# Wider score tiles, a split value product and one load moved up in a fused attention and SwiGLU kernel

## The chip, the cores and the metric

The kernel runs on one core of one Trainium2 chip. Its metric is the device time of one execution in microseconds, from the median of several runs. Five engines work side by side: PE (TensorE: matmuls, and their weight loads, which the profile lists apart as PEld), DVE (VectorE), ACT (ScalarE), POOL (GpSimd) and SP (SyncE). POOL also issues the loads, and SP the transposing copies and the stores.

## The reference

Softmax attention over 8 batches, 12 heads, 448 positions and head size 64, and then a gated feed-forward block over the 3584 resulting rows of 768 channels. Inputs and output are float32; the kernel computes with float16 operands and float32 accumulation.

```python
def _attn_ref(q, k, v):                      # (8, 12, 448, 64) each
    scores = np.matmul(q, k.transpose(0, 1, 3, 2)) / np.sqrt(q.shape[-1])
    scores = scores - np.max(scores, axis=-1, keepdims=True)
    attn = np.exp(scores)
    attn = attn / (np.sum(attn, axis=-1, keepdims=True) + 1e-09)
    return np.matmul(attn, v)

def _moe_ref(x, w_gate, w_val, w_out):       # x (3584, 768); 768 -> 1536 -> 768
    g = x @ w_gate
    silu = g * (1.0 / (1.0 + np.exp(-g)))
    return silu * (x @ w_val) @ w_out
```

## The kernel before

**Pairs, chunks and visits.** Heads are taken in 48 pairs, six pairs to a batch. A pair's scores are built transposed, keys on the partitions. For the pairs 0 to 11 the 448 keys are four chunks of 112 (`qk`, L234: two matmuls per chunk, one per head, 64 rows by 128 columns of weights). From pair 12 (`SPLIT`) on they are three chunks of 128 keys (`qk_split`, L249), and a remaining 64 keys. The remainders of two neighbouring pairs share one tile, called the rest (`qk_rest`, L265): the first 64 of its partitions hold the first half of the queries, the other 64 the second half. Each score tile is turned into `E` by one exponential on ACT.

After six pairs in an opening loop, the program runs through 54 *visits* that a list `plan` fixes. A visit issues up to three chunks, then what is due of an older couple of pairs (`todo`), and then feed-forward steps of an earlier batch. From pair 12 on, two kinds are due for each couple: "sums" (softmax sums, then reciprocals on DVE) and "both" (the value products of both pairs). For "both", `pv_rest` (L281) starts the two accumulators `acc[0]` and `acc[1]`, one for each half of the queries, and `pv_split` (L297) adds the three chunks to the first half and then to the second, each followed by a scaling on DVE into `X` (`scaled_half`, L312).

**Column tiles.** `qk_split` writes its 128 output partitions in four column tiles of 32: eight matmuls of 64 rows by 32 columns for a chunk, with a weight load for each; `qk_rest` has sixteen. In a visit with something due, the feed-forward matmuls are split by four in the same manner (`mm`, L396, under `tiled[0]`), and show as 128\*32 on line L401. In the other visits they are whole (128\*128, L398). The sums and value products are 128\*32 always.

**Feed-forward.** One step of `ffn1_steps` is a gate group `gp` in a buffer of the pool `ps_s` (3 buffers, shared with the score tiles), a tanh on ACT, a value group `vp` in a buffer of `ps_f` (2 buffers, shared with `acc` and `op`), and two products on DVE. `run_fv` runs such a step in its two halves. `ffn2_steps` gives the projection groups `op`: in the first block all three groups with the first half of the output weights (`wo[0]`), and then three with the second (`wo[1]`). A new block's steps are added by `add_block` in the visits in which its batch's last value product is made.

**Loads.** POOL issues them in program order. `wq` tells at which pair's visit the early ones are issued: the third group of values and `wo[0]` at pair 6, `wo[1]` at pair 7. From pair 8 on, each even pair loads q and k of the two pairs that are six further (`load_qk16`, `LA = 6`), so pair 8 loads 14 and 15, in four DMAs on line L136. `prep(pr + 3)` arranges a pair's q and k on POOL (L196 for pair 11, four copies on L182 from pair 12 on) and has SP transpose them into `qkT` (L199, L186). `double_rest` (L157) copies a part of the values on POOL. Each load on POOL's queue waits for the landing of the one eight before it.

```python
        wq = {
            0: [("qk", 6), ("g", 0), ("v", 0)],
            1: [("qk", 8), ("g", 1), ("v", 1)],
            3: [("qk", 10), ("V", 2), ("g", 2), ("v", 2)],
            4: [("g", 3), ("v", 3), ("qk", 12)],
            6: [("V", 3), ("o", 0)],
            7: [("o", 1)],
        }
```

The visits that matter most below, by the time of their first score matmul in the profiled execution: visit 8 at 63.07 us (chunks of pair 11), visit 9 at 69.17 (the last chunk of pair 11, two of pair 12), visit 10 at 72.89 (one of pair 12, two of 13), visit 11 at 79.36 (the last of 13, the rest, the first of 14), visit 12 at 84.51 (two of 14, the first of 15), visit 14 at 100.38.

Of the kernel before, what the change touches and what calls it, by code (L numbers as in the profile page):

```python
# [20 lines left out]
LA = 6  # L21
# [8 lines left out]
def kernel(  # L30
# [11 lines left out]
    B, H, S, D = q.shape  # L42
# [7 lines left out]
    NPAIR = B * NHP  # L50
# [4 lines left out]
    H2 = S // 2  # L55
    RS = 64
# [189 lines left out]
            )  # L246
        nc.scalar.activation(E[pr][:, c], s[0:P, :, 0:S], AF.Exp, scale=sm_scale)  # L247

    def qk_split(pr, c):  # L249
        if c == 0:  # L250
            E[pr] = ep.tile([128, NC, 2, S], FP16, tag="E", name="E")
        t = qkT[pr]
        s = ps_s.tile([128, 2, 512], FP32, tag="s")
        for j in range(4):
            for hx in range(2):
                nc.tensor.matmul(  # L256
                    s[ts(j, 32), hx, 0:S],
                    lhsT=t[ts(hx, 64), c, ts(j, 32)],
                    rhs=t[ts(hx, 64)].rearrange("p c q -> p (c q)")[:, S : 2 * S],
                    start=True,  # L260
                    stop=True,
                )
        nc.scalar.activation(E[pr][:, c], s[:, :, 0:S], AF.Exp, scale=sm_scale)  # L263

    def qk_rest(p0):  # L265
        s = ps_s.tile([128, 2, 512], FP32, tag="s")
        for i in range(2):
            t = qkT[p0 + i]
            for j in range(4):
                half = j // 2  # L270
                for hx in range(2):
                    nc.tensor.matmul(
                        s[ts(j, 32), hx, ds(i * H2, H2)],
                        lhsT=t[ts(hx, 64), 3, ds(j % 2 * 32, 32)],
                        rhs=t[ts(hx, 64)].rearrange("p c q -> p (c q)")[:, ds(S + half * H2, H2)],
                        start=True,
                        stop=True,
                    )
        nc.scalar.activation(E[p0 + 1][:, 3], s[:, :, 0:S], AF.Exp, scale=sm_scale)  # L279
# [14 lines left out]
                    )  # L294
        return acc

    def pv_split(p0, acc):  # L297
        for half in range(2):
            for c in range(3):
                for t in range(2):  # L300
                    for j in range(4):
                        g, r = divmod(p0 + j // 2, GP)
                        nc.tensor.matmul(  # L303
                            acc[half][ts(j, 32), ds(t * H2, H2)],
                            lhsT=v16[g][:, 2 * r + j % 2, c + 1, :].rearrange("p (d t) -> p t d", t=2)[:, t],
                            rhs=E[p0 + j // 2][:, c, j % 2, ds(half * H2, H2)],
                            start=False,
                            stop=(c == 2 and t == 1),
                        )
            scaled_half(p0, half, acc[half])  # L310

    def scaled_half(p0, half, acc):  # L312
        b, hp = divmod(p0, NHP)
        kk, bb = divmod(b, NB)
        if kk not in X:
            X[kk] = xp.tile([128, NCB, NB * S], FP16, tag="X", name="X")
        nc.vector.tensor_tensor(  # L317
            X[kk][:, hp : hp + 2, ds(bb * S + half * H2, H2)],
            acc[:, 0:S].rearrange("p (t q) -> p t q", t=2),
            R[p0][:, ds(half * H2, H2)].unsqueeze(1).to_broadcast([128, 2, H2]),  # L320
            ALU.mult,
        )
# [170 lines left out]
    def block(i):  # L493
        kk, odd = divmod(i, 2)
        c0, n = (384, 512) if odd else (0, 384)
        hts = hp_.tile([128, NFB, 512], FP16, tag="h")
        return ffn1_steps(kk, c0, n, hts), ffn2_steps(kk, c0, n, hts, i == 0, i == B - 1), n

    with tc.manual_schedule():
# [21 lines left out]
            3: [("qk", 10), ("V", 2), ("g", 2), ("v", 2)],  # L521
            4: [("g", 3), ("v", 3), ("qk", 12)],
            6: [("V", 3), ("o", 0)],
            7: [("o", 1)],
        }

        def emit(item):
# [10 lines left out]
        def pop_deferred(n=1):  # L538
            for _ in range(n):
                if deferred:  # L540
                    deferred.pop(0)()

        fvq = []
        oq = []
        count = {}

        def add_block(i, visits):
            f1, f2, n = block(i)
            oq.extend(ffn2_wait)
            ffn2_wait.clear()  # L550
            fvq.extend([(f1, NCB * n / 2400.0)] * NFB)
            own = [(f2, NFB * OH / 2400.0)] * (2 * (n // 128))
            (oq if i == 0 else ffn2_wait).extend(own)
            count.update(visits=visits, fv=NFB, o=len(oq), at=0, more=NFB - visits)

        def run_fv():
            gen, t = fvq.pop(0)
            for _ in range(2):
                next(gen)
                pop_deferred()  # L560
            return 2 * t

        def run_o():
            gen, t = oq.pop(0)
            next(gen)
            pop_deferred(2)
            return t

        def run_budget(budget):
            while (fvq or oq) and budget > 0:  # L570
                budget -= run_fv() if fvq else run_o()
            return budget
# [7 lines left out]
        for pr in range(FIRST):  # L580
# [24 lines left out]
            if pr in (2, 4):  # L605
                pop_deferred(1)
                halves = [pv(pr - 2, 0)]
# [4 lines left out]
        halves = [pv(p4, t) for t in range(2)]  # L612
# [3 lines left out]
        for p0 in range(FIRST, NPAIR, 2):  # L616
            at = len(units)
# [9 lines left out]
        while g < len(units) or queue:  # L627
            n = 2 if g < (WIDE - FIRST) * NC else 3
            todo = []
# [11 lines left out]
        def product(kind, p0):  # L641
            if kind == "sums":
                pop_deferred(99)
                deferred.extend(recips(p0, sums(p0)))
            elif kind == "both":
                pop_deferred(99)
                pv_split(p0, rests.pop(p0))
            else:
                if kind == 0:
                    pop_deferred(99)  # L650
                scaled(p0, kind, pv(p0, kind))

        def score(pr, c):
            if c == "rest":
                qk_rest(pr)
            elif pr >= SPLIT:
                qk_split(pr, c)
            else:
                qk(pr, c)

        rests = {}

        carry = 0.0
        for x, (chunks, todo) in enumerate(plan):
            for pr, c in chunks:
                score(pr, c)
            for _, kind, p0 in todo:
                if kind == "both":
                    rests[p0] = pv_rest(p0)
            end = min([y for y in adds if y > x] + [len(plan) + 1])  # L670
            if x == 0:
                for t in range(2):
                    scaled(p4, t, halves[t])
                add_block(0, end)
            turn2 = None
            entered = [pr for pr, c in chunks if c == 0]
            for pr in entered:
                if pr >= SPLIT:
                    double_rest(pr)
                if NPE <= pr + 3 < NPAIR:  # L680
                    prep(pr + 3)
                if pr % 2 == 0 and 14 <= pr + LA < NPAIR:
                    load_qk16(pr + LA)
                if pr % GP == 0 and 4 <= pr // GP + 1 < NGRP:
                    load_v(pr // GP + 1)
            for pr, c in chunks:
                if c == 2 and pr < NPE - 2:
                    prep(pr + 2)()
            any_p = len(todo)
            if x in adds and x > 0:  # L690
                while todo:
                    product(*todo.pop(0)[1:])
                add_block(adds[x], end - x)
            while todo:
                product(*todo.pop(0)[1:])
            for pr in entered:
                for w in wq.pop(pr, []):
                    emit(w)
            tiled[0] = bool(any_p) and (not chunks or chunks[0][0] >= TILED)
            if adds[max(y for y in adds if y <= x)] < 2:  # L700
                carry = run_budget(left() / (end - x) + carry)
            else:
                at, n = count["at"], count["visits"]
                no = share(count["o"], at, n)
                nf = 1
                if no and count["more"] > 0:
                    o_left = sum(1 for y in range(at, n) if share(count["o"], y, n))
                    extra = -(-count["more"] // o_left)
                    nf += extra
                    count["more"] -= extra  # L710
                count["at"] += 1
                for step in range(no if not any_p else 0):
                    run_o()
                for y in range(nf):
                    if fvq:
                        run_fv()
                for _ in range(no if any_p else 0):
                    run_o()
            tiled[0] = False
        run_budget(1e9)  # L720
        pop_deferred(99)
        add_block(B - 1, 1)
# [33 lines left out]
```

The softmax here doesn't subtract the row's maximum and nothing guards it: scores larger than these inputs give would overflow.

## Time and profile before

| what | value |
|---|---|
| time, median of 6 runs (lowest to highest) | 463.03 us (461.44 to 466.65) |
| profiled execution, its own time | 463.45 us |
| its span, first to last instruction | 461.6 us |
| instructions in the span | 19197 |
| PE busy | 445.1 us (96%) |
| DVE, ACT, POOL busy | 238.4, 227.1, 152.3 us |
| granted TensorE clock, mean | 0.998 |

The span is 1.85 us shorter than the time of that execution. PE is busy nearly all the time, so what counts is where it isn't, and the steps between its groups of matmuls. A line of the profile names the engine and the source line, what is written and read, and the shape: "64\*32 64x448" is a matmul with 64 rows and 32 columns of weights and 448 columns streamed. "Idle before, releaser" tells what ended the engine's wait; "issue" means that nothing that the profile shows was waited for.

### The profile page before, as it was taken

What the parts mean: (1) busy time and instruction counts of PE and PEld (TensorE: products, weight loads), DVE (VectorE), ACT (ScalarE), POOL (GpSimd) and SP (SyncE); (2) the same over time, 40 slices, a digit from 0 to 9 for tenths busy, and PEclk for the clock granted to TensorE, in tenths of its full rate; (3) what the DMA queues carried; (4) which work ended last, traced back from release to release, by engine and by line L of the source; (5) the groups of instructions that cost most, each with busy time, mean ns of one, the idle gap of its engine ahead of it and who ended that gap; (6) DMA issues with size and microseconds to landing.
All of it is one profiled execution on the core that took longest, in us unless ns stands there. A gap on an engine that the chain in (4) does not pass through costs nothing.

```text
span 461.6 us, 19197 instructions
## 1 busy us (share of the span) xinstructions
PE 445.1 (96%) x8816; PEld 259.8 (56%) x8816; DVE 238.4 (52%) x374; ACT 227.1 (49%) x335; POOL 152.3 (33%) x320
## 2 busy tenths in 40 slices
PE   8899998979999999999999999999999999999996
PEld 3355555455456676565557665555546666544564
DVE  2765763547476545746366374566357455354200
ACT  6986656535545445545353455633545542222222
POOL 8554806945536061811527125520400000000000
PEclk9999999999999999999999999999999999999999
DMA  9999999997847166933919639743322102100133
GB/s 131 195 200 201 188 178 148 214 147 88 103 70 99 46 94 110 145 45 77 141 35 119 98 59 136 111 49 77 44 64 58 27 14 70 36 1 0 36 103 104
DMA packets 86289, 44.57 MB, mean 97 GB/s; under 512 B 51264, under 2 KB 82752, under 8 KB 86208
## 3 DMA queue, kind: packets, MB, share of 16 engines
q0 software_dynamic: 46592, 23.37, 41.9%
q1 hardware_dynamic: 39376, 19.77, 23.9%
q8 instruction: 69, 1.13, 1.0%
q10 hardware_dynamic: 240, 0.20, 0.1%
q14 instruction: 12, 0.10, 0.1%
HBM read 47.19 MB, written 11.01 MB: 126 GB/s over the span
## 4 chain that ended last, share of the span: by engine, by line
PE 80%; DMA 13%; POOL 2%; issue 1%; DVE 1%; ACT 1%; ACTq 0%; POOLq 0%
PE vp L401 15%; PE gp L401 15%; PE op L401 13%; PE op L398 8%; PE gp L398 6%; PE vp L398 6%; PE acc L303 5%; PE s L256 5%; DMA wg<-in_moe_w_gate_dram 5%; DMA k<-in_k_dram 5%; PE acc L362 3%; DMA wv<-in_moe_w_val_dram 3%; PE acc L288 1%; DMA qkT<-qk 1%; PE wp L107 1%
## 5 line engine op out<-in xcount | busy, mean ns | idle before, releaser
L429 DVE SCALAR_TENSOR_TENSOR t<-sg,gp 128x384 f32<-128x384 f32 (+1 forms) x96 | 58.7, 612 | 98.6 <-ACT sg L417 98.6
L417 ACT ACTIVATE sg<-gp 128x384 f32<-128x384 f32 (+1 forms) x96 | 52.5, 547 | 97.6 <-PE gp L401 63.9
L263 ACT ACTIVATE E<-s 128x896 f16<-128x896 f32 x108 | 92.7, 921 | 15.1 <-PE s L256 14.8
L401 PE MATMUL gp<-X,wg 128*32 128x384 f16 (+1 forms) x1632 | 89.4, 350 | 0.7 <-issue 0.4
L401 PE MATMUL vp<-X,wv 128*32 128x384 f16 (+1 forms) x1632 | 88.8, 349 | 0.0
L462 ACT ACTIVATE osb<-op 128x384 f32<-128x384 f32 (+1 forms) x57 | 27.8, 488 | 106.8 <-PE op L401 81.8
L401 PE MATMUL op<-wo,hts 128*32 128x384 f16 x1728 | 77.2, 326 | 1.3 <-issue 0.9
L386 DVE RECIPROCAL R<-ssb 128x112 f32<-128x112 f32 x92 | 73.5, 829 | 0.8
L432 DVE SCALAR_TENSOR_TENSOR hts<-t,vp 128x384 f16<-128x384 f32 (+1 forms) x96 | 59.6, 621 | 11.2 <-DVE t L429 1.4
L401 PEld LDWEIGHTS <-wv 128*32 128x32 f16 x1632 | 47.3, 97 | 29.0 <-issue 0.3
L401 PEld LDWEIGHTS <-hts 128*32 128x32 f16 x1728 | 49.7, 97 | 24.0 <-issue 2.3
L401 PEld LDWEIGHTS <-wg 128*32 128x32 f16 x1632 | 46.0, 97 | 26.2 <-issue 2.1
L136 POOL DMA_DIRECT2D vt<-in_v_dram x24 | 16.0, 675 | 117.9 <-PE acc L303 117.9
L247 ACT ACTIVATE E<-s 112x896 f16<-112x896 f32 x48 | 40.4, 924 | 6.7 <-PE s L240 6.3
L398 PE MATMUL op<-wo,hts 128*128 128x384 f16 (+1 forms) x252 | 40.2, 319 | 0.0
L398 PE MATMUL gp<-X,wg 128*128 128x512 f16 (+1 forms) x168 | 37.7, 360 | 0.7 <-ACT E L279 0.7
L398 PE MATMUL vp<-X,wv 128*128 128x512 f16 (+1 forms) x168 | 37.6, 360 | 0.0
L182 POOL COPY qk<-k 128x384 f16<-128x384 f16 x72 | 28.7, 398 | 24.4 <-DMA qkT<-qk 22.5
L383 DVE COPY ssb<-acc 128x448 f32<-128x448 f32 x23 | 14.4, 624 | 38.7 <-PE acc L371 31.9
L317 DVE TENSOR_TENSOR X<-acc,R 128x448 f16<-128x448 f32 x36 | 21.7, 625 | 23.2 <-PE acc L303 23.2
L256 PE MATMUL s<-qkT 64*32 64x448 f16 x864 | 30.0, 353 | 3.8 <-issue 2.3
L398 PEld LDWEIGHTS <-hts 128*128 128x128 f16 x252 | 23.9, 98 | 16.0 <-issue 1.7
(60 smaller groups left out, 352.7 us busy)
## 6 DMA issues: line engine op xcount, KB each, us to landing
out_dram<-osb SPq DMA_DIRECT2D x42, 192.0 KB, 2.7
wg<-in_moe_w_gate_dram POOLq DMA_DIRECT2D x8, 288.0 KB, 11.1
wv<-in_moe_w_val_dram POOLq DMA_DIRECT2D x8, 288.0 KB, 11.4
q<-in_q_dram POOLq DMA_DIRECT2D x18, 128.0 KB, 4.4
k<-in_k_dram POOLq DMA_DIRECT2D x18, 128.0 KB, 5.7
wo<-in_moe_w_out_dram POOLq DMA_DIRECT2D x2, 1152.0 KB, 18.6
vt<-in_v_dram POOLq DMA_DIRECT2D x12, 192.0 KB, 5.2
q<-in_q_dram POOLq DMA_DIRECT2D x18, 96.0 KB, 4.0
```

What stands on the lines that cost most here:

```text
L182: nc.gpsimd.tensor_copy(qk7[rows, c0 : c0 + n].rearrange("p c h d -> p h c d"), src[rows, :, x0 : x0 + n])
L247: nc.scalar.activation(E[pr][:, c], s[0:P, :, 0:S], AF.Exp, scale=sm_scale)
L256: nc.tensor.matmul(s[ts(j, 32), hx, 0:S], lhsT=t[ts(hx, 64), c, ts(j, 32)], rhs=t[ts(hx, 64)].rearrange("p c q -> p (c q)")[:, S : 2 * S], ...
L263: nc.scalar.activation(E[pr][:, c], s[:, :, 0:S], AF.Exp, scale=sm_scale)
L303: nc.tensor.matmul(acc[half][ts(j, 32), ds(t * H2, H2)], lhsT=v16[g][:, 2 * r + j % 2, c + 1, :].rearrange("p (d t) -> p t d", t=2)[:, t], ...
L386: lambda i=i: nc.vector.reciprocal(rt[:, ts(i, P)], ssb[:, ts(i, P)]) for i in range(4)
L398: nc.tensor.matmul(dst, lhsT=lhsT, rhs=rhs, start=start, stop=stop)
L401: nc.tensor.matmul(dst[ts(j, 32), :], lhsT=lhsT[:, ts(j, 32)], rhs=rhs, start=start, stop=stop)
L417: nc.scalar.activation(sg[:, 0:n], gp[:, 0:n], AF.Tanh, scale=0.5)
L429: nc.vector.scalar_tensor_tensor(t1[:, 0:n], sg[:, 0:n], 1.0, gp[:, 0:n], ALU.add, ALU.mult)
L432: nc.vector.scalar_tensor_tensor(hts[:, fb, 0:n], t1[:, 0:n], 0.5 * HS, vp[:, 0:n], ALU.mult, ALU.mult)
L462: nc.scalar.activation(osb[:, ds(m0, w)], op[:, 0:w], AF.Copy, scale=1.0 / HS)
```

## The change

It has three parts. The column tiles of `qk_split` and `qk_rest` get a width per visit: 32 where a "both" is due, else 64 where the visit has a rest, else 128. The second half of `pv_split` is no longer issued right after the first: it is put in a list `second` and issued behind the next gate group (or by `finish()`, where a block is added, where no feed-forward step follows, and at the end of a visit). And q and k of the pairs 14 and 15 are loaded at pair 7, with `wo[1]` moved to pair 8.

```diff
-    def qk_split(pr, c):
+    def qk_split(pr, c, cols):
...
-        for j in range(4):
+        for j in range(128 // cols):
             for hx in range(2):
                 nc.tensor.matmul(
-                    s[ts(j, 32), hx, 0:S],
-                    lhsT=t[ts(hx, 64), c, ts(j, 32)],
+                    s[ts(j, cols), hx, 0:S],
+                    lhsT=t[ts(hx, 64), c, ts(j, cols)],
...
-    def qk_rest(p0):
+    def qk_rest(p0, cols):
...
-            for j in range(4):
-                half = j // 2
+            for j in range(128 // cols):
+                half, at = divmod(j * cols, RS)
                 for hx in range(2):
                     nc.tensor.matmul(
-                        s[ts(j, 32), hx, ds(i * H2, H2)],
-                        lhsT=t[ts(hx, 64), 3, ds(j % 2 * 32, 32)],
+                        s[ts(j, cols), hx, ds(i * H2, H2)],
+                        lhsT=t[ts(hx, 64), 3, ds(at, cols)],
...
-    def pv_split(p0, acc):
-        for half in range(2):
+    def pv_split(p0, acc, halves):
+        for half in halves:
...
-            7: [("o", 1)],
+            7: [("qk", 14)],
+            8: [("o", 1)],
...
             for _ in range(2):
                 next(gen)
+                while second:
+                    second.pop()()
                 pop_deferred()
...
-                pv_split(p0, rests.pop(p0))
+                acc = rests.pop(p0)
+                pv_split(p0, acc, (0,))
+                second.append(lambda: pv_split(p0, acc, (1,)))
...
+        def finish():
+            while second:
+                second.pop()()
...
+            cols = 64 if any(c == "rest" for _, c in chunks) else 128
+            if any(kind == "both" for _, kind, _ in todo):
+                cols = 32
             for pr, c in chunks:
-                score(pr, c)
+                score(pr, c, cols)
...
-                if pr % 2 == 0 and 14 <= pr + LA < NPAIR:
+                if pr % 2 == 0 and 16 <= pr + LA < NPAIR:
                     load_qk16(pr + LA)
...
+                finish()
                 add_block(adds[x], end - x)
...
+                if not fvq or not nf:
+                    finish()
...
             tiled[0] = False
+            finish()
```

More of the change, by code (lines that the diff above doesn't have):

```diff
@@ L541, in pop_deferred @@
                     deferred.pop(0)()
+        second = []
         fvq = []
@@ L651, in product, with score @@
                 scaled(p0, kind, pv(p0, kind))
-        def score(pr, c):
+        def finish():
+            while second:
+                second.pop()()
+        def score(pr, c, cols):
             if c == "rest":
-                qk_rest(pr)
+                qk_rest(pr, cols)
             elif pr >= SPLIT:
-                qk_split(pr, c)
+                qk_split(pr, c, cols)
             else:
```

## The prediction

> **What bounds the kernel now.** First the page's busy row: PE fills 96% of the span, no other engine more than 52%. So time is gained or lost only where PE stands still, or between its groups. The DMA row shows the engines nearly full for nine slices (some 104 us), then not.
>
> ```profile
> PE 445.1 (96%) x8816; PEld 259.8 (56%) x8816; DVE 238.4 (52%) x374; ACT 227.1 (49%) x335; POOL 152.3 (33%) x320
> ...
> DMA  9999999997847166933919639743322102100133
> ```
>
> Next, PE's waits from 60 to 112 us, where the moved load acts. Three carry the case: one for pair 14's `qkT`, two for "issue".
>
> ```profile
> PE s L256 <- issue: 2.3, 1, 2.3
> PE s L256 <- DMA qkT<-qk: 1.4, 1, 1.4
> PE acc L288 <- DVE hts L432: 0.7, 2, 0.4
> PE op L401 <- issue: 0.7, 1, 0.7
> ```
>
> The chain of waits shows where pair 14 was held up: its last k load is issued at 52.66, behind both output-weight loads, and lands at 74.38; the copies follow, the transpose lands at 81.33, and PE starts at once.
>
> ```profile
> 47.68 2.05 POOL wo L170 x2
> ...
> 52.66 21.72 DMA k<-in_k_dram
> 74.59 1.20 POOL qk L182 x3
> 76.16 5.17 DMA qkT<-qk
> ```
>
> Last, PE's timeline at the 2.3 us "issue" wait: it stops after 7 of a chunk's 8 matmuls, with every operand there.
>
> ```profile
> 100.38 0.38 PE L256 MATMUL s<-qkT 64*32 64x448 f16 x7
> 103.10 0.72 PE L256 MATMUL s<-qkT 64*32 64x448 f16 x17 [2.34 <-issue]
> ```
>
> Counting PE's and PEld's records, this stop is before number 3263. Four more such stops end at 76.67, 94.44, 254.00 and 258.27, at numbers 2239, 3007, 10175 and 10431: all leave 191 when divided by 256. The trace also has instruction packets of 16384 bytes on queue 8 (at 74.32, 92.05, 99.92, 251.52, 255.94), and each stop ends 1.3 to 1.7 us after one has finished. So PE runs out of instructions at a 256-instruction boundary when that packet comes late. Against undisturbed spacing the five cost 0.85 + 0.31 + 2.53 + 0.43 + 0.60 = 4.7 us.
>
> **The change, part by part.** *Wider tiles.* By the visit list, 56 chunks in 19 visits go from 8 matmuls to 2; in 7 visits 12 chunks go to 4, and 7 rests from 16 to 8. With their weight loads that is 672 + 96 + 112 = 880 fewer of 17638 PE instructions. Does the array gain? The trace has both widths beside 32-column work:
>
> ```profile
> 54.12 0.74 PE L240 MATMUL s<-qkT 64*128 64x448 f16 x6
> 54.80 0.94 PE L335 MATMUL acc<-E,vt 112*32 112x448 f16 x16
> ...
> 314.29 0.76 PE L256 MATMUL s<-qkT 64*32 64x448 f16 x24
> 314.98 0.75 PE L362 MATMUL acc<-E,ones 128*32 128x448 f16 x12
> ```
>
> Three chunks take 0.68 us wide and 0.69 narrow: the eight narrow matmuls already run at once. A change of shape costs 0.10 to 0.12 us beyond the last group's streaming (into 64\*128: 0.11, into 64\*32: 0.11, out: 0.105 and 0.115). Worth 0.01 us in each of 26 visits, plus one change of shape (0.107) that goes in visit 9, where pairs 11 and 12 now have one width: -0.35 us. No trace row has 64\*64 in this use; between its two neighbours it lies at nothing, and I bound it at +-0.05 us in 7 visits, +-0.35. A rule speaks against wide tiles: the Trainium skill, "TensorE: Matmul & The Clock Gate", section "LDWEIGHTS (loading the stationary operand)", gives columns/1.2 ns, so 107 ns for 128 columns against 27 for 32. With no matmul in flight to hide it after a change of shape, 19 x 80 + 7 x 27 ns = +1.7 us (an estimate from that page). The rows say 93 ns for a 64x128 load and 90 for a 64x32, and the first matmul starts 5 ns after the first load in both. I take the rows: nothing.
>
> *Instructions.* This is where the width can pay. "Runtime: NRT & Kernel Launch", section "Instruction fetch mechanics", calls a 16 KiB boundary mostly hidden; by that, 880 instructions are worth nothing. The trace puts 4.7 us on five boundaries. Fewer instructions mean 3.4 of 69 boundaries less, which alone is 0.2 us; but they also move the boundaries and spread them over more time. At the 100 us stop, 164 instructions are saved by then, so the boundary falls into visit 14's feed-forward, some 3.7 us of work later, while the packet is asked for (when the previous boundary is passed) only 2.9 us later. At 76 us, 60 saved put it 1.2 us later. Deferring half of a value product helps the same way: 48 instructions in 0.58 us move behind a gate group that uses 48 in 0.97 to 1.29. Bounds: -4.7 (all gone) and +2 (as many stops as before, and one of the longest size nearly added). I take -2.6: most of the three stops before 104 us (-3.0), half of the two at 254 and 258 (-0.5), and +0.9 for new ones.
>
> *Second half behind a gate group.* No matmul is added, and no shape changes, since a "both" visit's feed-forward is 128\*32 too. The 0.58 us of the second half gave cover: the gate group takes the buffer of the visit's first score tile, whose exponential ends 0.14 us before the second half starts (in 14 of 17 visits; more in the others). A release takes 0.05 us, so the gate group, 0.58 us earlier, still has 0.09 to spare. `acc[1]` is freed some 1 to 1.3 us later; the next user of its buffer is the second value group, which starts 1.9 us or more after that half. Only where one step is followed by `op` (visits 50 and 53) it is nearly even: 0.05 each. DVE's scaling of the second half is ahead of the step's two products, as before. POOL's value loads wait for these products (117.9 us in all, 9 times), with transposes behind them in POOL's queue; but from pair 16 on a transpose lands 11 us or more before its use, so 1.3 us hurts nobody. In the five visits that add a block nothing is deferred. Sum: 0.
>
> *Pair 14's loads.* Four DMAs (two q, two k) go ahead of `wo[1]`, and with it ahead of pair 11's two POOL copies. What becomes early: after `wo[0]` (62.0, from 47.68 + 14.3 us to landing) the four take 74.38 - 71.7 = 2.7 us, so pair 14 lands at 64.7 instead of 74.4, and its 1.62 us stall (1.44 in the wait list, with the step into the group) can go. What becomes late:
> - Pair 11's copies. The four issues cannot start before 48.7, and the second must wait for the load eight before it (landed at 49.7). They end at 51.7, the copies at 52.9: the transpose is issued 2.0 us later than 50.93. It landed 1.88 us ahead of its use: a stall of about 0.2.
> - The transposes of 12 and 13 come 0.8 us later from POOL and follow in SP's queue, where they landed 5.5 us apart while `wo` was moving. Pair 13 had 0.83 us to spare: 0 to 1.3, I take 0.6.
> - `wo[1]` lands 2.7 us later, at 74.4, and pair 14's transpose now shares its transfer (a transpose alone takes 2.9 us): 74.4 to 77.3. The fourth projection, its first user, started at 74.35, and at 75.0 with the two stalls above: 0 to 2.3, I take 0.2.
> - Pair 14 itself, behind 13 in SP's queue, lands near 79.4, when PE comes for it. Pair 15 waits, in POOL's order, for a `double_rest` that needs values loaded behind `wo[1]`; its transpose landed at 84.31 with 0.59 to spare, and PE would come 0.5 to 1.5 us sooner: +0.3.
> Sum: -1.62 + 0.2 + 0.6 + 0.2 + 0.3 = -0.3, with ends at -1.6 and +3.
>
> Total: -0.35 - 2.6 + 0 - 0.3 = -3.25 us. The profiled execution took 463.45 us (span 461.6), 0.42 over the median of 463.03; the stalls are counted in that execution, so I subtract from it: 460.2 us.
>
> **The rivals.** *B: the stops only move.* Boundaries come as often within 5%, and DMA stays full until 104 us, so other groups are hit for the same 4.7 us. For it: the stops at 254 and 258 lie where DMA is not full. Against: the long one depends on one packet in one jam. 463.45 - 0.65 = 462.8.
>
> *C, slower: the transposes and `wo[1]` come late.* Place: PE at the fourth projection. `wo[1]` was 23.0 us on its way; issued at 52.9 it would land at 75.9, and with pair 14's transpose inside at 78.8. For it: transposes issued during `wo` took 10.3, 12.0 and 14.5 us, against a median of 5.2. Against: the bytes ahead of it grow by 2.7 us only. With the stalls of 11 and 13 grown to 1.4 together, PE would come at 75.6 and wait 3.2: 1.4 + 3.2 - 1.62 - 0.35 = +2.6, and with the instruction stops merely moved 466.1. It decides once `wo[1]` lands about 1.2 us after PE has come for it, stops unchanged.
>
> *D: gate groups wait for the score buffer.* If exponentials end over 0.09 us later than now in the 13 deferred visits, each waits; 0.3 each is +3.9: 464.1. Against: chunks, shapes and ACT's order in those visits are unchanged.
>
> *E: all goes well.* Pair 14's stall goes without a new one, the stops nearly vanish: 463.45 - 0.35 - 1.6 - 4.0 = 457.5.
>
> **How the numbers follow.** The forecast 0.47, B 0.22, C 0.12, D 0.07, E 0.12. Faster by over 0.5% means under 460.7, slower over 465.3 (half a percent is about what a measurement of this kernel can tell from no change). The forecast lies just under that bound: 0.39 of it faster, 0.08 same. E is faster; B and D are same, with 0.02 of them slower; C is 0.11 slower and 0.01 same. Faster 0.51, same 0.36, slower 0.13. The range from 457.4 to 465.0 leaves out most of C and the outer half of E.
>
> **What would show it.** Right: 480 matmuls on L256 (now 864) and 232 on L272 (now 288), 16758 PE instructions; pair 14's score chunk without a DMA wait near 79 us; "issue" waits of PE under 2.5 us in sum; the PE groups of sums visits with unchanged spacing; no PE wait of `gp` for `E`. Wrong: an "issue" wait of over 2 us anywhere before 110; `op` L401 waiting for `wo`, or `s` for `qkT`, by over 1.5 us in sum between 60 and 90 us; shape changes into or out of 64\*128 or 64\*64 of over 0.15 us.

## The result: 0.23% faster, where 0.6% was forecast as likeliest

The changed kernel takes 460.7 us (median of 35 runs) beside 461.82 for the kernel before (72 runs, which hold the six shown at first): a ratio of 0.9977, 95% interval 0.9964 to 0.9990. That is faster by more than its own noise, 1.1 us, and less than the 2.8 us that the forecast put between its 460.2 and the first median. The two first profiled executions lie further apart, 463.45 and 460.47 us (spans 461.6 and 458.7), and that difference is a part of the answer. All ratios, intervals and counts of clocks leave out the few slow runs, over 1.5% above the fastest of their kernel. A ratio is not the quotient of the medians shown.

The page's busy and DMA rows after the change: 440 matmuls and as many weight loads fewer, the same work on the other engines, and DMA engines full for about as long.

```profile
PE 444.3 (97%) x8376; PEld 257.1 (56%) x8376; DVE 237.6 (52%) x374; ACT 226.5 (49%) x335; POOL 152.3 (33%) x320
...
DMA  9999999998678086934839558823323102100143
```

PE's waits from 60 to 112 us after the change. PE still waits for `qkT`, now twice, and the two "issue" waits have become one of 0.3.

```profile
PE s L256 <- DMA qkT<-qk: 1.3, 2, 0.7
PE acc L288 <- DVE hts L432: 0.7, 2, 0.4
PE vp L401 <- issue: 0.3, 1, 0.3
PE op L401 <- DVE X L349: 0.3, 1, 0.3
```

PE's timeline says whose transposes these are. At 74.03 it is pair 13, at 84.36 pair 15; pair 14's first chunk at 80.15 runs without a wait.

```profile
72.92 0.36 PE L256 MATMUL s<-qkT 64*128 64x448 f16 x2
74.03 0.55 PE L256 MATMUL s<-qkT 64*128 64x448 f16 x4 [0.74 <-DMA qkT<-qk]
...
80.15 0.36 PE L256 MATMUL s<-qkT 64*64 64x448 f16 x4
...
84.36 0.36 PE L256 MATMUL s<-qkT 64*128 64x448 f16 x2 [0.54 <-DMA qkT<-qk]
```

The chain shows why 15 is late. Pair 14's last k load lands at 66.07, 8.3 us earlier than before, and its copies follow at once. Then POOL stands for 8.44 us, until the values behind the second output weights land and the copy on L157 can run; pair 15's copies are behind it.

```profile
51.46 14.61 DMA k<-in_k_dram
...
66.28 1.20 POOL qk L182 x3
...
67.82 8.44 issue
...
76.28 0.30 POOL vt L157
76.63 1.20 POOL qk L182 x3
...
78.20 6.11 DMA qkT<-qk
```

POOL's timeline names the landing that the chain shows as "issue":

```profile
76.28 0.29 POOL L157 COPY vt<-vt 64x128 f16<-64x128 f16 x1 [8.46 <-DMA vt<-in_v_dram]
```

A sums visit with wide tiles, to be held against the two timelines of before: three chunks and the change of shape take 0.67 us.

```profile
311.38 0.74 PE L256 MATMUL s<-qkT 64*128 64x448 f16 x6
312.05 0.75 PE L362 MATMUL acc<-E,ones 128*32 128x448 f16 x12
```

And the longest stop of PE in this execution, now at 197 us, inside a gate group that the second half of a value product follows at 198.13:

```profile
195.41 0.39 PE L401 MATMUL gp<-X,wg 128*32 128x512 f16 x3
197.04 1.46 PE L401 MATMUL gp<-X,wg 128*32 128x512 f16 x21 [1.24 <-issue]
198.13 0.75 PE L303 MATMUL acc<-E,vt 128*32 128x224 f16 x22
```

Counted as in the prediction (records of PE and PEld in order, the excess over undisturbed spacing wherever the number leaves 191 when divided by 256), the stops of this execution are 0.29, 0.51 and 1.41 us, 2.2 in sum, where the first profile of before had 4.7.

That these stops are late instructions can be tested on all 14 profiles listed below. The packets of 16384 bytes on queue 8 are counted in order, and each is set beside its own boundary: packet 1 beside number 447, packet 2 beside 703, and so on by 256. PE passes 917 such boundaries, and never sooner than 1.22 us after the end of the boundary's own packet. Each of the 56 stops there that cost over 0.15 us ends 1.2 to 1.9 us after that packet.

### The profile page after: what moved, and what is told of

It reads as the page before. It is cut to its first block, busy times and chain, and to the rows that moved or that the text cites. A ratio compares the mean times of both kernels' runs of the same rounds, so it can differ in the third digit from the quotient of the medians.

```text
span 458.7 us, 18316 instructions
## 1 busy us (share of the span) xinstructions
PE 444.3 (97%) x8376; PEld 257.1 (56%) x8376; DVE 237.6 (52%) x374; ACT 226.5 (49%) x335; POOL 152.3 (33%) x320
## 4 chain that ended last, share of the span: by engine, by line
PE 80%; DMA 12%; issue 3%; ACT 2%; DVE 1%; POOL 1%; ACTq 0%; POOLq 0%
PE vp L401 15%; PE gp L401 15%; PE op L401 13%; PE op L398 8%; PE gp L398 6%; PE vp L398 6%; PE acc L303 5%; PE s L256 5%; DMA k<-in_k_dram 3%; PE acc L362 3%; DMA wv<-in_moe_w_val_dram 3%; DMA q<-in_q_dram 3%; DMA vt<-in_v_dram 2%; ACT E L247 1%; DMA qkT<-qk 1%
## 5 line engine op out<-in xcount | busy, mean ns | idle before, releaser
L401 PE MATMUL gp<-X,wg 128*32 128x384 f16 (+1 forms) x1632 | 89.3, 350 | 1.5 <-issue 1.2
L401 PE MATMUL vp<-X,wv 128*32 128x384 f16 (+1 forms) x1632 | 89.0, 349 | 0.3 <-issue 0.3
L401 PE MATMUL op<-wo,hts 128*32 128x384 f16 x1728 | 76.9, 326 | 0.4 <-DVE X L349 0.3
L401 PEld LDWEIGHTS <-hts 128*32 128x32 f16 x1728 | 49.7, 97 | 22.9 <-issue 1.4
L401 PEld LDWEIGHTS <-wv 128*32 128x32 f16 x1632 | 46.1, 97 | 28.7 <-issue 0.8
L401 PEld LDWEIGHTS <-wg 128*32 128x32 f16 x1632 | 45.2, 97 | 27.9 <-issue 2.9
L256 PE MATMUL s<-qkT 64*32 64x448 f16 (+2 forms) x480 | 29.5, 353 | 1.3 <-DMA qkT<-qk 1.3
```

The costliest lines, as they stand in the source:

```text
L256: nc.tensor.matmul(s[ts(j, cols), hx, 0:S], lhsT=t[ts(hx, 64), c, ts(j, cols)], rhs=t[ts(hx, 64)].rearrange("p c q -> p (c q)")[:, S : 2 * S],
L401: nc.tensor.matmul(dst[ts(j, 32), :], lhsT=lhsT[:, ts(j, 32)], rhs=rhs, start=start, stop=stop)
```

## The experiments

Ratios are against the kernel before, run beside each: its median was 462.28 us beside before2, after2, width_only and load_only, 462.31 beside width_defer, defer_only, copies_first and width_defer_shift, and 462.52 beside before_shift, after_shift, width_defer_shift_again and width_defer_shift2. So medians of different rows are not to be compared. The shifted versions with wide tiles have 7 to 9 runs each, the others 14 to 35. Columns on the right come from one profiled execution each: the stops at instruction boundaries, and the waits between 60 and 90 us for a transpose or for the second output weights (both as excess over undisturbed spacing, which is up to 0.3 us more than the wait that a view shows).

| kernel | median us | ratio, 95% interval | stops, us | data waits, us |
|---|---|---|---|---|
| before, first profile | 461.82 | 1 | 4.7 | 1.6 |
| before2 | 462.84 | 1.0006 (0.9984 to 1.0027) | 3.8 | 1.1 |
| defer_only | 462.18 | 1.0000 (0.9985 to 1.0014) | 3.3 | 1.3 |
| load_only | 464.29 | 1.0046 (1.0027 to 1.0066) | 5.1 | 3.8 |
| before_shift | 463.49 | 1.0017 (0.9997 to 1.0036) | 8.7 | 0.2 |
| after, first profile | 460.70 | 0.9977 (0.9964 to 0.9990) | 2.2 | 1.6 |
| after2 | 460.95 | 0.9975 (0.9954 to 0.9997) | 7.6 | 0.6 |
| width_only | 462.20 | 0.9988 (0.9963 to 1.0013) | 2.4 | 2.5 |
| width_defer | 461.46 | 0.9969 (0.9948 to 0.9991) | 3.9 | 2.5 |
| copies_first | 462.15 | 0.9992 (0.9969 to 1.0015) | 1.1 | 4.2 |
| after_shift | 459.79 | 0.9955 (0.9932 to 0.9978) | 1.3 | 0.8 |
| width_defer_shift | 458.26 | 0.9937 (0.9913 to 0.9961) | 1.4 | 1.5 |
| width_defer_shift_again | 459.56 | 0.9931 (0.9905 to 0.9956) | 0.6 | 1.6 |
| width_defer_shift2 | 460.30 | 0.9946 (0.9914 to 0.9978) | 1.8 | 2.0 |

**before2 and after2: the same two kernels, profiled again.** No edit.

> The kernel before, unchanged, for a second profile. Theory (the record's sum is right in kind, but the profiled execution before was an unlucky one): PE's instruction stops, 4.7 us in the first profile, come out nearer to 3 us here, still at numbers that leave 191 when divided by 256; pair 14 again waits about 1.5 us for its transpose. Rival (the stops are a fixed cost of this program): again five stops at the same five numbers, 4.7 us within 0.3.

> The changed kernel, unchanged, for a second profile. Theory: stalls for the transposes of pairs 13 and 15 again, 1.6 us in sum, and instruction stops of 1 to 3 us at other places than in its first profile; time 0.1 to 0.4% under the kernel before. Rival (stops fixed): again 0.29, 0.51 and 1.41 us near 78, 97 and 197 us.

The stops came at the same five numbers in before2, but with other sizes: the one at number 3263 was 0.89 us instead of 2.53, the one at 2239 was 1.39 instead of 0.85. So the rival, a fixed cost of the program, is out. In after2 they are 7.6 us in sum, from 2.2; the profiled execution was 465.22 us, among the slowest of its 22. PE's waits from 60 to 300 us in after2:

```profile
PE vp L401 <- issue: 2.8, 2, 1.9
PE gp L401 <- issue: 1.7, 1, 1.7
PE op L401 <- issue: 1.3, 1, 1.3
```

So the numbers at which a stop can fall are the same in every profile; how long it is differs from one execution to the next by as much as 1.6 us (at 3263 before, at 3007 after). One profile is one draw. The theory's 1 to 3 us for after2 was too narrow, and pair 13's stall didn't come back (its transpose landed 0.48 us ahead of its use).

**width_only.** The load order and the value products are put back:

```diff
-            7: [("qk", 14)],
-            8: [("o", 1)],
+            7: [("o", 1)],
...
-                pv_split(p0, acc, (0,))
-                second.append(lambda: pv_split(p0, acc, (1,)))
+                pv_split(p0, acc, (0, 1))
```

(with `14 <= pr + LA` as in the kernel before.)

> Only the column tiles get their width by the visit; value products whole, loads in the old order. Theory (width is what pays, by shape changes and fewer instructions): -0.35 us from shape changes and 0.5 to 1.5 us from stops, so 0.2 to 0.4% faster; the stall of pair 14 (1.5 us) stays. Rival (the gain is the load's): no difference, within 0.1%.

Inconclusive: 0.12% faster, with an interval that holds no gain as well as 0.37%. The wait for pair 14 was 2.4 us here, and in 8 of its 14 runs the mean granted clock was 0.997 or less (the last section shows where that is lost), in the kernel before in 25 of 152.

**load_only.** Of the change only the load order is kept; `cols = 32` in all visits, value products whole.

> Only pair 14's loads go ahead of the second output weights; score tiles all 32 wide, value products whole. Theory: pair 14's stall of 1.6 us is replaced by stalls for 13 (0.9) and 15 (0.7) and perhaps 0.2 for 11: time the same within 0.15%. Rival (the gain is the load's): 0.2 to 0.4% faster.

Slower by 0.46%, so neither the theory nor its rival. POOL's timeline shows what the four issues of pair 14 do to pair 11's copies (L196): the second q load waits 1.41 us for the load eight before it, and the copies start at 53.07, where they started at 49.72 in the kernel before.

```profile
48.18 1.03 POOL L170 DMA_DIRECT2D wo<-in_moe_w_out_dram  x1 [1.30 <-issue]
49.21 0.63 POOL L136 DMA_DIRECT2D q<-in_q_dram  x1
51.26 0.61 POOL L136 DMA_DIRECT2D q<-in_q_dram  x1 [1.41 <-DMA wv<-in_moe_w_val_dram]
51.86 1.23 POOL L136 DMA_DIRECT2D k<-in_k_dram  x2
53.07 0.64 POOL L196 COPY qk<-q 112x512 f16<-112x512 f16 x1
```

PE's waits from 60 to 112 us show what it cost: 1.9 for pair 11, and 1.4 for the pairs 13 and 15.

```profile
PE s L256 <- issue: 2.6, 1, 2.6
PE s L240 <- DMA qkT<-qk: 1.9, 1, 1.9
PE s L256 <- DMA qkT<-qk: 1.4, 2, 0.8
```

Pair 14 no longer waits. In the changed kernel's own two profiles pair 11 came through with 0.66 and 1.32 us to spare. Here it did not: the transpose was issued 1.0 to 1.3 us later still, at 54.28, and took 10.7 us to land where it had taken 9.2 in both.

**width_defer.** The change without the load's part.

> Widths by visit and the split value product, loads in the old order. Theory: 0.2 to 0.4% faster than the kernel before, so as good as the whole change or better, with pair 14's stall of 1.1 to 1.6 us still there. Rival (the load carries the gain): no faster than the kernel before.

0.31% faster, as good as the whole change. The load adds nothing to the time that could be measured, though pair 14 waits 2.2 us in this profile. It may show in the clock: 8 of 20 runs here had a mean granted clock of 0.997 or less, of the changed kernel's 56 only 2.

**defer_only.** Of the change only the second half is moved.

> Only the second half of the value products goes behind the first gate group; tiles 32 wide, loads in the old order. Theory: no wait of a gate group for E, none of a projection for acc, shape changes and instruction count as before, stops at the same numbers and of 3.8 to 4.7 us: time the same within 0.15%. Rival (spreading the instructions thins the stops): 0.2% or more faster, with the stops at 254 and 258 us gone.

No difference, to within 0.15%, and no new wait. Between 60 and 300 us the list of PE's waits has none of a gate group of the tiled visits (L401) for `E`, and none of a projection for the split product's `acc`. The one wait of a gate group for `E` is that of a whole group, which the kernel before has too:

```profile
PE gp L398 <- ACT E L279: 0.7, 1, 0.7
```

The stops, 3.3 us, came out under the 3.8 to 4.7 expected. Of the two late ones one was absent (254 us), the other 0.61 us.

**copies_first.** Pair 14's loads back at pair 8, behind pair 11's copies, with the second output weights still behind them:

```diff
-            7: [("qk", 14)],
             8: [("o", 1)],
...
-                if pr % 2 == 0 and 16 <= pr + LA < NPAIR:
+                if pr % 2 == 0 and 14 <= pr + LA < NPAIR:
```

> The changed kernel with one order mended: pair 14's loads stay at pair 8, where pair 11's copies go ahead of them, and the second output weights follow at pair 8. Theory (the moved load was paid for by pair 11's copies standing behind its four issues): pair 11's transpose is issued near 51 us again instead of 53.3, lands before its use with over 1 us to spare, pair 13's stall (0.9) goes, pair 14's stays away, and 0.5 us or so is left at pair 15: 1 us faster than the changed kernel, 0.4 to 0.5% faster than the kernel before. Rival (the transposes are held up by the weights' traffic alone, whatever POOL's order): pair 13 waits as in the changed kernel, time equal to it.

The theory's first steps hold: pair 11's transpose is issued at 50.87, the pairs 11, 13 and 14 do not wait. But the time is that of the kernel before, not 0.4 to 0.5% under it. The second output weights were issued at 53.77 and landed at 77.78, and the fourth projection waited for them; then pair 15 was 2.0 us late. PE's waits from 60 to 112 us:

```profile
PE op L401 <- DMA wo<-in_moe_w_out_dram: 2.1, 1, 2.1
PE s L256 <- DMA qkT<-qk: 1.8, 1, 1.8
```

This is the place of the prediction's rival C, in another kernel. With its 1.1 us of stops, the fewest but one, it still gained nothing. Its matmuls stand in the same order as those of the changed kernel and of width_defer. Yet the boundary at which three profiles of those two stopped for 1.4 to 1.9 us, inside the gate group at 197 to 200 us (number 7359), was passed without a stop in this execution:

```profile
198.38 1.61 PE L401 MATMUL gp<-X,wg 128*32 128x512 f16 x24
```

**width_defer_shift, and the same again.** The start's dummy matmuls are cut in four. The columns streamed stay the same, and 72 instructions more stand ahead of all else:

```diff
-        for _ in range(n):
-            nc.tensor.matmul(wp[:], lhsT=warm[:, 0:128], rhs=warm[:], start=True, stop=True)
+        for _ in range(4 * n):
+            nc.tensor.matmul(wp[:, 0:128], lhsT=warm[:, 0:128], rhs=warm[:, 0:128], start=True, stop=True)
```

> As width_defer, with the twelve dummy matmuls of the start cut in four each (128 columns instead of 512), which adds 72 PE instructions ahead of everything else: every instruction boundary moves 72 instructions earlier in the work. Theory (the stops are a lottery of boundary against traffic): the stops come at other places of the work, their sum changes by 1 to 2 us either way against width_defer, and the time with it, while waits for data stay. Rival (stops sit where DMA is jammed, wherever the boundary falls): the sum stays within 0.5 us.

> The fastest version once more, for more runs and a second profile. Theory: 0.4 to 0.7% faster than the kernel before, stops of under 2 us in sum, none near 199 us. Rival (its few runs were lucky): 0.3%, as width_defer.

0.63% and 0.69% faster than the kernel before: the best version here, and better than the changed kernel, whose interval ends at 0.36%. Laid beside each other matmul by matmul, the profile of width_defer_shift ends 3.4 us ahead of that of width_defer: it gains 1.9 at 199 us, 1.75 between 92 and 98 and about 1 around 80 and 84, loses 0.9 at 102 and 0.7 at 303 to its own stops, and keeps step elsewhere to 0.4 us. So nearly all of the difference is stops and data waits. The stop that cost width_defer 1.8 us at 199 us is absent. PE's timeline there, of width_defer:

```profile
197.23 0.39 PE L401 MATMUL gp<-X,wg 128*32 128x512 f16 x3
199.28 1.05 PE L401 MATMUL gp<-X,wg 128*32 128x512 f16 x16 [1.66 <-issue]
```

and of width_defer_shift, at the same group, whole:

```profile
194.79 0.65 PE L303 MATMUL acc<-E,vt 128*32 128x224 f16 x20
195.27 1.47 PE L401 MATMUL gp<-X,wg 128*32 128x512 f16 x24
```

In the second profile of it the longest wait from 60 to 300 us is that for pair 14 (1.3 us); the one "issue" wait in that list is 0.4.

**width_defer_shift2.** `8 * n` dummies of 64 columns: 168 instructions more.

> As width_defer, with each dummy cut in eight (64 columns): +168 instructions. Theory (lottery): a third set of stops, at places of the work that neither width_defer nor width_defer_shift has; their sum anywhere from 1 to 5 us, and a time from 0.1 to 0.6% under the kernel before. Rival (cutting the dummies helps by itself): as fast as width_defer_shift or faster, with the start ending earlier.

0.54% faster. One stop of 1.8 us at 100.7 us, none near 199; pair 15 waited 1.9. The start ends no earlier.

**before_shift.** The same cut into four in the kernel before.

> The kernel before with the start's twelve dummy matmuls cut in four each (+72 PE instructions ahead of all else, the array's time the same). Theory (a lottery of boundary against traffic): the boundary that stopped PE at 101 to 103 us falls 72 instructions earlier in the work, into the last value group before it, with the same traffic: a stop there of 1 us or more again; time the same within 0.2%. Rival (cutting the dummies helps by itself): 0.3% faster or more.

No gain; if anything slower. So the cut dummies do not help by themselves. The stop near 102 us was 3.5 us long (2.53 and 0.89 in the two profiles without the cut), and others came at 76, 198, 202 and 296 us. Its waits from 60 to 300 us:

```profile
PE gp L401 <- issue: 3.6, 2, 3.4
PE acc L303 <- issue: 1.4, 2, 0.8
PE acc L362 <- issue: 1.0, 1, 1.0
```

**after_shift.** The cut into four in the changed kernel.

> The changed kernel with the same 72 instructions more. Theory: the stop near 197 to 200 us (1.4 and 1.9 us in the two profiles of the changed kernel) is gone, as in width_defer_shift; the stalls of pairs 13 and 15 stay; 0.2 to 0.4% under the changed kernel, 0.4 to 0.6% under the kernel before. Rival (the width and the deferral carry it, not the boundaries): time equal to the changed kernel, 0.2% under the kernel before.

0.45% faster than before, as the theory had it, and the stop near 197 us is absent. The interval holds the changed kernel's own ratio (0.9977), so the rival, that it is no faster than that kernel, is not excluded. Pair 13's stall was absent in this execution, pair 15's was 0.8 us.

## Why the prediction was right, and where its sum was not

The range and the direction held, and the likeliest time of 460.2 us was 0.5 off. That closeness is luck: the sum started 1.6 us too high, at the time of one execution, and took 2.1 us too much off, 3.25 where the change took 1.1. Point by point:

*Wider tiles on the array: -0.35.* Right in kind. Into 64\*128 costs 0.11 us as before; out of it into 128\*32 costs 0.095 where 64\*32 cost 0.115; 64\*64 into 128\*128 costs 0.105, so the unseen shape lies between its neighbours. The change of shape in visit 9 is gone. That sums to -0.5 us. (The prediction's own terms give 0.37, not 0.35; and its "5 ns in both" holds for the wide visit at 54.12, while in the narrow one at 314.29 the first matmul starts 1 ns after its load.) The Trainium skill's rule for weight loads, as the prediction works it out, would have put +1.7 here; no such cost is in the trace.

*Instructions: -2.6. This is the step that failed, as a size.* The counts came as forecast (480 matmuls on L256, 232 on L272). Its sign of being right, "issue" waits under 2.5 us in sum, held in the first profile and not in after2, where the list above has 5.8. Against the first pair of profiles it looks perfect, 4.7 to 2.2. But 4.7 was one execution's draw, which stood 1.6 us above the median that 72 runs later gave; I subtracted from it as if the stops were the program's. Without the cut dummies the draws are 3.3, 3.8, 4.7 and 5.1 us in four profiles with narrow tiles (mean 4.2), and 1.1, 2.2, 2.4, 3.9 and 7.6 in five with the widths of the change (mean 3.4): 0.8 less, and the groups overlap. With the cut they are 8.7 in the one narrow profile, and 0.6, 1.3, 1.4 and 1.8 in four wide ones. In times, width and deferral together gave 0.31%, 1.4 us, of which some 0.5 is changes of shape. What is left for the stops is about 1 us, by subtraction and with an interval of about 0 to 2, not 2.6. Rival B, that they only move, put 462.8 against the first median of 463.03, a gain of 0.2; that is nearer to the measured 1.1 than the forecast's 2.8.

*That PE stops for late instructions at a boundary* is shown: by the 917 boundaries and their packets. *That the place of the boundaries is worth time* is shown less well. The stop near 199 us is absent in all four shifted profiles, but of four unshifted ones with the same order of matmuls copies_first has none there either. In times, 72 instructions took 0.2 to 0.4% off the kernels with wide tiles (each against its own unshifted ratio, with intervals that overlap) and nothing off the one with narrow tiles. A part of that may be the clock's: a mean granted clock of 0.997 or less is found in 8 of 20 runs of width_defer and in 1 of 23 of its shifted forms. That fewer instructions, and not the widths in another way, thin the stops is argued from the counts; no kernel had wide tiles with the old number of instructions.

*Second half behind a gate group: 0.* Shown by defer_only: 1.0000, interval 0.9985 to 1.0014. The 0.09 us of spare time for the score buffer was enough; rival D did not occur.

*Pair 14's loads: -0.3.* The exchange was foreseen. In the first profile after: pair 14's 1.62 is gone, 0.91 for pair 13 (I had 0.6) and 0.70 for pair 15 (0.3) came, 0 for pair 11 (0.2) and 0 for the weights (0.2; they landed at 74.75, and PE came at 75.28). Net 0.0. Pair 11's transpose was issued at 53.29; the working had 52.9. What I had too small was the risk: alone, on a POOL that was a microsecond later, this part cost 0.46%, 2.1 us, as much as the data waits of that profile grew (3.8 from 1.6). The bounds of -1.6 and +3 held that.

*What binds the stretch.* Across all versions the data waits between 60 and 90 us are 0.2 to 4.2 us, whichever load goes first: pair 14 alone, or 13 and 15, or 11, 13 and 15, or the weights and 15. The DMA row is full there in both kernels. Reordering picks who waits; no order tried here made the waits vanish. Whether less traffic would was not tried.

## What to carry to other kernels

When PE stops in the middle of a group with every operand there, number its instructions: if the stops all leave the same remainder at 256, as here, hold them against the instruction packets. If late packets explain them, fewer instructions, or a few dummy ones ahead of all else, are worth a trial of their own (here the dummies went with a gain in the wide kernels and none in the narrow one). Take their size from several profiles before it is subtracted from anything. And a load moved forward on a queue delays the small work behind it: in load_only four issues of 0.6 us and one wait of 1.41 for an old landing cost more than the transfer that they brought forward, and in the changed kernel as much.

## What the runs showed of the hardware that was not expected

With 72 instructions more at the very start, for the same columns streamed, two versions of a 460 us kernel took 0.2 to 0.4% less; how much of that is the instructions' is open, as said above.

A long wait of PE can cost more than itself. In width_only the wait for pair 14 (2.23 us at 81.22) was followed by ten sets of four projection matmuls at doubled spacing, about 0.155 us extra each, 1.5 us in sum. In this table the busy times of PE, PEld, DVE, ACT and POOL are followed by the granted clock: 0.57 between 82 and 86 us.

```profile
79.00:82.00 3.00, 0.79 (x16) 0.43 (x20) 0.00 (x0) 1.92 (x4) 2.99 (x5) 1.00 0.96 131
82.00:86.00 4.00, 4.00 (x60) 1.95 (x52) 0.63 (x1) 0.63 (x1) 3.67 (x11) 0.57 1.49 183
86.00:90.00 4.00, 4.00 (x82) 2.10 (x82) 2.01 (x3) 3.27 (x5) 3.84 (x9) 1.00 1.03 207
```

The same followed the 2.8 us stop in load_only (1.5 us more), but not the 3.5 us stop of before_shift or the 2.2 us waits of copies_first. No run tried what decides, but the traces fit one reading. In all 14 the granted clock changes only at whole multiples of 3.413 us from its first rise to full speed, and within the work it stays at half for one such stretch. In width_only PE stood still for 2.20 us of the stretch before (79.02 to 82.43), in load_only for 1.94 (103.11 to 106.52). The 3.5 us stop of before_shift lies across two stretches, 1.77 and 1.58 us in each, and the waits of copies_first fill 1.56 of theirs. Of all stretches up to 455 us, one more was followed by half clock, with 2.00 us (width_defer_shift_again, at the end); those without it reach 1.94 (load_only, at 62.15) and 1.93. So a wait seems to cost extra where well over half of one stretch is idle; the limit near 1.94 us rests on three cases.
